# Chunked attention and a gated feed-forward block: eleven small copies behind one sigmoid, and two subtractions in another place of the plan

## The chip, the cores and the metric

The kernel runs on one core of a Trainium2 chip. The metric is the device time of one execution in microseconds (us), the median of several runs. TensorE is written PE (its weight loads PEld), VectorE DVE, ScalarE ACT, GpSimd POOL, and the queue that issues the transfers SP.

## The reference: what is computed

Attention within chunks of 64 tokens (8 batches, 8 heads, 576 tokens, heads of 64), and behind it a gated feed-forward block on 4608 tokens with 512 features and 1536 hidden features, all in 32-bit floats:

```
scores = scale * matmul(q_c, k_c^T);  scores -= max(scores)
attn = exp(scores) / (sum(exp(scores)) + 1e-9);  x = matmul(attn, v_c)
out = (sigmoid(x @ w_gate) * (x @ w_val)) @ w_out
```

The weights arrive as 64-bit floats and are converted on the chip.

## The kernel before, in words

The 4608 tokens are nine blocks of 512. Every matrix product is made of three products of reduced-precision parts: each operand is split into a high part (a rounded copy) and a low part (the difference from it), and high·high, high·low and low·high are added up. Block 0 and the conversion of the weights follow a list written out by hand. Blocks 1 and 2 are worked by `rest` (line 893), one hidden slice of 128 features after the other: `step` calls `hidden` (line 369), and `finish` calls `down` for the slice before. Blocks 3 to 8 are worked two at a time by `pairs` (line 915), where a scheme of seven products takes the place of eight, so that sums and differences of the input tiles are needed (`differ`, line 508, and `operands`, line 515).

In one slice of blocks 1 and 2 PE does twelve matmuls for the gate (bank g0), twelve for the value (bank g1), and twelve of `down` for the slice before. Gate and value have the same name, g, and the same line 356 in the profile. Behind the gate ACT takes the sigmoid into hf (L372); behind the value DVE multiplies (L375), ACT rounds the product into hx (L378), and DVE writes the low part of hx (L380). The gate of the next slice can begin only when the sigmoid has read g0, its value only when the multiplication has read g1.

Beside this runs the attention of later blocks. It is a generator, `flow` (line 757), whose pieces `tick` lets out one by one. A piece is bought with credit, and some wait on a word: "apart" holds the generator while the tick's place is "middle", and where blocks are not yet joined in pairs also until a tick after the one at which the word came up; "piece" holds it for a tick in a like way. A pass of the attention on two heads goes: scores on PE (sc, L196), the maximum and the subtraction on DVE (L782, L783), the exponential on ACT (L787, which changes ACT's table before and after it), sum, reciprocal and product on DVE (L805 to L810), two transposes on DVE (L814). The transposed 32-wide blocks are then put in place by sixteen copies (L825, pr to pt): every third one is POOL's, at once, and the other eleven are ACT's. In blocks 1 and 2 these eleven are not written at once but put on a list, `held`, and `release` writes them out. When all sixteen are there, PE multiplies them with the values (av, L211). `release(5)` writes the first five of the list, `release()` up to sixteen.

Engines run their instructions in the order in which they are written. That order is fixed by hand for all engines in blocks 0 to 2 but for POOL and SP in part, and for PE and POOL in the pairs, where the compiler's scheduler sets the others. During blocks 1 and 2 POOL and DVE also make sums of weight parts (a_val, a_high, L451 to L465), which SP writes to memory for the pairs.

In the pairs a product pair is `first` (products into cx and cy, then s1u = cy + copy of cx on DVE, L568), `last` of the pair before (L622, L625), and `middle` (L601, L607, and the multiplications L578). Product 7 of `middle` adds into the same bank cy that L568 reads. Product 5 of `middle` is written to bank g0 (cz), the bank that L622 of the pair before has to read first.

Of the kernel before, what the change touches and what calls it, by code (L numbers as in the profile page):

```python
# [68 lines left out]
def chunk_attn_moe(ctx: ExitStack, tc: tile.TileContext, q, k, v, w, out, outt):  # L69
# [278 lines left out]
    def up(m, f, which, tok):  # L348
        ps = ps_g.tile([P, TB], F32, tag=f"g{which}", name=f"g{which}", bufs=1)
        n = 0  # L350
        for u in range(2):
            x = xt[m, u]
            for i in range(2):
                c = (2 * u + i) * P
                for wpart, part in ((0, 0), (0, 1), (1, 0)):
                    nc.tensor.matmul(  # L356
                        ps[:, tok], lhsT=wt[f, which][:, wpart, c:c + P], rhs=x[:, part, i, tok],
                        start=n == 0, stop=n == 11)
                    n += 1
        return ps[:, tok]  # L360
# [3 lines left out]
    def release(most=16):  # L364
        for one in held[:most]:
            one()
        del held[:most]

    def hidden(m, f, tok):
        pg = up(m, f, 0, tok)  # L370
        hf = mp.tile([P, TB], F32, name="hf", bufs=1)[:, tok]
        nc.scalar.activation(hf, pg, AF.Sigmoid)  # L372
        release(5)
        pv = up(m, f, 1, tok)
        nc.vector.tensor_tensor(out=hf, in0=pv, in1=hf, op=ALU.mult)  # L375
        both = mp.tile([P, 2, TB], F32R, name="hx")
        hh, hl = both[:, 0], both[:, 1]
        nc.scalar.copy(hh[:, tok], hf)  # L378
        release()
        nc.vector.tensor_tensor(out=hl[:, tok], in0=hf, in1=hh[:, tok].bitcast(F32), op=ALU.subtract)  # L380
        return m, f, tok, hh, hl
# [126 lines left out]
    def differ(n):  # L508

        for (u, b), (u0, b0), (u1, b1) in (((0, 1), (0, 1), (0, 0)), ((1, 1), (1, 1), (0, 1))):  # L510
            yield 1.2
            nc.vector.tensor_tensor(
                out=raw[n, u][:, :, b], in0=raw[n, u0][:, :, b0], in1=raw[n, u1][:, :, b1], op=ALU.subtract)

# [242 lines left out]
    def flow():  # L757
# [3 lines left out]
        for j in range(8, 4 * NB + 2, 2):  # L761
# [34 lines left out]
            if n > 0 and rest == 0:  # L796
                yield from differ(n - 1)
                yield ("early", n - 1)
                yield from operands(n - 1)
                yield ("up", n - 1)  # L800
# [76 lines left out]
    def step(m, f, span):  # L877
        pending.append(hidden(m, f, spans[span]))
# [114 lines left out]
```

## Time and profile before

| | |
|---|---|
| runs | 901.86, 905.09, 906.74 us, median 905.09 |
| the profiled execution | 902.03 us, of which 900.2 us lie between its first and its last instruction |
| PE busy | 98% of the span; DVE 69%, ACT 46%, POOL 30% |
| PE's granted clock | 0.996 of full speed over the span |
| blocks 1 and 2 | from about 150 to 357 us |
| the three pairs | from about 357 us on |

A matmul's duration in the trace overlaps the next one's, so a stretch of PE is read by the distance between starts. "Idle before" in brackets is the time the engine stood still before the row, with the instruction that ended it.

### The profile page before, as it was taken

The numbers are of one execution on the slowest core, as the hardware profiler recorded it, in microseconds if no ns is written. First come the engines' busy times: TensorE is split into PE (matmuls) and PEld (weight loads), VectorE is DVE, ScalarE is ACT, GpSimd is POOL, SyncE is SP. The second block draws the span as 40 slices with busy tenths as digits, with TensorE's granted clock in tenths as the row PEclk, the third lists the DMA queues.
The fourth block names the chain that finished last, engine by engine and source line by source line (L and its number), as shares of the span: only waits on it lengthen the run. The fifth ranks groups of instructions, "written<-read, shape, count | busy, mean of one in ns | idle before, by whom it ended". The sixth has DMA issues, their size and how long they took to land.

```text
span 900.2 us, 15612 instructions
## 1 busy us (share of the span) xinstructions
PE 882.1 (98%) x6054; PEld 720.3 (80%) x6054; DVE 618.8 (69%) x882; ACT 412.0 (46%) x738; POOL 272.4 (30%) x337
## 2 busy tenths in 40 slices
PE   7999999999999999999999999999999999999998
PEld 4887788887877878888888888887788888888886
DVE  6999882586665966666658976666679853435884
ACT  7887672355524463355544524455246221122341
POOL 0000000397846990267750001253500002432000
PEclk9999999999998999999999999999999999999999
DMA  8899962336354475588775567665446685564553
GB/s 312 305 338 297 353 195 71 131 129 190 131 166 148 142 221 177 171 278 284 257 277 187 210 231 283 234 234 190 163 160 224 211 283 197 183 204 150 187 210 117
DMA packets 84506, 189.77 MB, mean 211 GB/s; under 512 B 7248, under 2 KB 45648, under 8 KB 80592
## 3 DMA queue, kind: packets, MB, share of 16 engines
q1 hardware_dynamic: 84432, 188.77, 61.2%
q8 instruction: 48, 0.79, 0.4%
q14 instruction: 26, 0.21, 0.1%
HBM read 146.28 MB, written 42.47 MB: 210 GB/s over the span
## 4 chain that ended last, share of the span: by engine, by line
PE 81%; DVE 7%; ACT 4%; POOL 3%; issue 2%; DMA 2%; SPq 0%; POOLq 0%; DVEq 0%; ACTq 0%
PE d L699 19%; PE g L356 16%; PE cy L550 15%; PE cx L550 11%; PE cz L550 10%; PE acc L391 7%; PE av L211 2%; PE sc L196 2%; DMA w_raw<-w_in 2%; POOL pt L825 1%; ACT early L263 1%; ACT pt L825 1%; POOL a_val L465 1%; DVE xc L540 1%; DVE w_raw L153 1%
## 5 line engine op out<-in xcount | busy, mean ns | idle before, releaser
L356 PE MATMUL g<-xt,w 128*128 128x512 f32 (+1 forms) x960 | 208.1, 372 | 1.0 <-ACT hf L312 0.5
L356 PEld LDWEIGHTS g<-xt,w 128*128 128x128 f32 x960 | 168.5, 190 | 34.1 <-ACT hf L312 1.5
L699 PE MATMUL d<-hd,wd 128*128 128x512 f32 x756 | 172.5, 389 | 0.1
L699 PEld LDWEIGHTS d<-hd,wd 128*128 128x128 f32 x756 | 141.7, 188 | 30.3 <-DVE hd L679 0.9
L550 PE MATMUL cy<-xc,wr 128*128 128x512 f32 x648 | 159.4, 389 | 1.2 <-DVE s1u L568 1.2
L550 PEld LDWEIGHTS cy<-xc,wr 128*128 128x128 f32 x648 | 121.6, 188 | 26.8 <-DVE s1u L568 1.6
L550 PE MATMUL cx<-xc,wr 128*128 128x512 f32 x432 | 111.0, 392 | 0.6 <-issue 0.6
L550 PE MATMUL cz<-xc,wr 128*128 128x512 f32 x432 | 110.0, 390 | 0.2
L391 PE MATMUL acc<-w,hx 128*128 128x512 f32 x432 | 106.7, 394 | 0.1
L550 PEld LDWEIGHTS cz<-xc,wr 128*128 128x128 f32 x432 | 80.9, 188 | 17.8 <-issue 1.0
L550 PEld LDWEIGHTS cx<-xc,wr 128*128 128x128 f32 x432 | 80.5, 188 | 18.0 <-issue 1.0
L391 PEld LDWEIGHTS acc<-w,hx 128*128 128x128 f32 x432 | 79.7, 188 | 17.7 <-DVE hx L322 0.8
L825 POOL COPY pt<-pr 32x256 f32<-32x256 f32 x94 | 39.7, 423 | 163.9 <-DVE pr L814 154.8
L460 POOL TENSOR_TENSOR a_val<-a_val 128x128 f32<-128x128 f32 x36 | 19.0, 527 | 217.9 <-DVE a_val L451 167.5
L678 ACT CAST hd<-hid 128x1024 fp32r<-128x1024 f32 x48 | 49.9, 1052 | 49.2 <-PE d L699 33.2
L566 ACT COPY s1u<-cx 128x512 f32<-128x512 f32 x36 | 21.1, 587 | 106.3 <-PE cx L550 106.3
L679 DVE TENSOR_TENSOR hd<-hid,hd 128x1024 fp32r<-128x1024 f32 x48 | 58.3, 1221 | 12.4 <-ACT hd L678 12.2
L578 POOL TENSOR_TENSOR hid<-u,hid 128x512 f32<-128x512 f32 x15 | 19.3, 1285 | 142.4 <-DVE u L607 141.7
L825 ACT COPY pt<-pr 32x256 f32<-32x256 f32 x130 | 52.4, 403 | 10.5 <-DVE pr L814 8.6
L568 DVE TENSOR_TENSOR s1u<-cy,s1u 128x512 f32<-128x512 f32 x36 | 24.7, 685 | 39.9 <-PE cy L550 35.4
L628 ACT ACTIVATE hid<-hid 128x512 f32<-128x512 f32 x54 | 32.4, 628 | 35.3 <-DVE hid L622 29.3
L578 POOL TENSOR_TENSOR hid<-s1u,hid 128x512 f32<-128x512 f32 x30 | 41.1, 1379 | 20.8 <-DVE s1u L622 20.2
(118 smaller groups left out, 1118.4 us busy)
## 6 DMA issues: line engine op xcount, KB each, us to landing
wr<-sums SPq DMA_DIRECT2D x72, 512.0 KB, 4.8
wd<-stream SPq DMA_DIRECT2D x30, 1024.0 KB, 4.6
w_raw<-w_in SPq DMA_DIRECT2D x36, 512.0 KB, 5.2
wr<-given SPq DMA_DIRECT2D x36, 512.0 KB, 3.8
qt<-q_in SPq DMA_DIRECT2D x18, 512.0 KB, 4.8
kt<-k_in SPq DMA_DIRECT2D x18, 512.0 KB, 5.7
vt<-v_in SPq DMA_DIRECT2D x18, 512.0 KB, 4.7
given<-w SPq DMA_DIRECT2D x36, 256.0 KB, 5.6
```

The costliest lines, as they stand in the source:

```text
L356: nc.tensor.matmul(ps[:, tok], lhsT=wt[f, which][:, wpart, c:c + P], rhs=x[:, part, i, tok], start=n == 0, stop=n == 11)
L391: nc.tensor.matmul(acc[m, t], lhsT=hx[:, ts], rhs=wt[f, 2][:, wpart], start=f == 0 and i == 0, stop=f == NF - 1 and i == 2,)
L460: nc.gpsimd.tensor_tensor(out=val[:, 1], in0=val[:, 1], in1=val[:, 2], op=ALU.add)
L550: nc.tensor.matmul(bank, lhsT=lhs(wpart, c), rhs=x[:, part, c], start=start and k == 0, stop=stop and k == 5, skip_group_check=True)
L566: nc.scalar.copy(s1, x)
L568: nc.vector.tensor_tensor(out=u2, in0=y, in1=s1, op=ALU.add)
L578: eng.tensor_tensor(out=h, in0=value, in1=h, op=ALU.mult)
L628: nc.scalar.activation(h, h, AF.Sigmoid)
L678: nc.scalar.copy(t[:, 0], at)
L679: nc.vector.tensor_tensor(out=t[:, 1], in0=at, in1=t[:, 0].bitcast(F32), op=ALU.subtract)
L699: nc.tensor.matmul(bank, lhsT=w[:, o:o + P], rhs=x[:, part], start=p == 0 and opening and i == 0, stop=p == 5 and i == 2, skip_group_check ...
L825: copy = (lambda eng, dst=pb[dst, :, c, i, :], src=ps[src, h::2, k, :]: eng(dst, src))
```

## The change

Two edits. In `hidden` the call behind the sigmoid releases the whole list instead of five copies; the call behind the rounding of hx stays and finds the list empty. In `differ` each of the two subtractions is held at places named "middle", and where blocks are not joined (the first pair's) also for one tick more.

```diff
@@ hidden(m, f, tok)
         nc.scalar.activation(hf, pg, AF.Sigmoid)
-        release(5)
+        release()
         pv = up(m, f, 1, tok)
         nc.vector.tensor_tensor(out=hf, in0=pv, in1=hf, op=ALU.mult)
...
@@ differ(n)
             yield 1.2
+            yield "apart"
             nc.vector.tensor_tensor(
                 out=raw[n, u][:, :, b], in0=raw[n, u0][:, :, b0], in1=raw[n, u1][:, :, b1], op=ALU.subtract)
```

The added line moves every later line of the file down by one. The order of instructions is the same on PE, POOL and SP. On ACT the copies move in six places, which look alike. One of them, in block 1, before the change; "pt<-pr" are the copies, "hx<-hf" is the rounding, L787 the exponential:

```order
L372 ACTIVATE hf<-g_2341 128x512
L825 COPY pt<-pr 32x8x32 x5
L378 CAST hx<-hf 128x512
L825 COPY pt<-pr 32x8x32 x6
L787 ACT_TABLE_LOAD
L787 ACTIVATE pr<-pr 128x1024
```

and the same place after it:

```order
L372 ACTIVATE hf<-g_2341 128x512
L826 COPY pt<-pr 32x8x32 x11
L378 CAST hx<-hf 128x512
L788 ACT_TABLE_LOAD
L788 ACTIVATE pr<-pr 128x1024
```

Six copies go from behind the rounding of hx to ahead of it.

On DVE the first pair's subtractions (L512) stand at the end of block 2 among the multiplications of its last slices (L375) and the work on the pair's operands (L528, L540). Before the change:

```order
L375 TENSOR_TENSOR hf<-g_3684,hf 128x512
L380 TENSOR_TENSOR hx<-hf,hx 128x512
L512 TENSOR_TENSOR raw<-raw 128x2x512 x2
L540 TENSOR_TENSOR xc<-raw,xc 128x1024 x3
L528 TENSOR_TENSOR raw<-raw 128x2x512
L375 TENSOR_TENSOR hf<-g_3754,hf 128x512
L380 TENSOR_TENSOR hx<-hf,hx 128x512
L540 TENSOR_TENSOR xc<-raw,xc 128x1024 x2
L528 TENSOR_TENSOR raw<-raw 128x2x512 x2
L375 TENSOR_TENSOR hf<-g_3806,hf 128x512
L380 TENSOR_TENSOR hx<-hf,hx 128x512
L540 TENSOR_TENSOR xc<-raw,xc 128x1024 x2
```

and after it:

```order
L375 TENSOR_TENSOR hf<-g_3684,hf 128x512
L380 TENSOR_TENSOR hx<-hf,hx 128x512
L513 TENSOR_TENSOR raw<-raw 128x2x512
L375 TENSOR_TENSOR hf<-g_3741,hf 128x512
L380 TENSOR_TENSOR hx<-hf,hx 128x512
L513 TENSOR_TENSOR raw<-raw 128x2x512
L541 TENSOR_TENSOR xc<-raw,xc 128x1024 x3
L529 TENSOR_TENSOR raw<-raw 128x2x512
L541 TENSOR_TENSOR xc<-raw,xc 128x1024 x2
L529 TENSOR_TENSOR raw<-raw 128x2x512
L375 TENSOR_TENSOR hf<-g_3803,hf 128x512
L380 TENSOR_TENSOR hx<-hf,hx 128x512
```

The second subtraction and what follows it come behind one more multiplication, and eight operations on whole operand tiles now stand between two multiplications, where four and four stood. ACT's roundings of these tiles move with them: five in a row ahead of a sigmoid, where four stood ahead of the sigmoid of one slice before.

The second pair's subtractions keep their place. The third pair's, on DVE in the last products of the second pair, before the change:

```order
L601 TENSOR_TENSOR u_6585<-cy,s1u_6480 128x512
L607 TENSOR_TENSOR hid<-cz,u_6585 128x512
L512 TENSOR_TENSOR raw<-raw 128x2x512 x2
L568 TENSOR_TENSOR s1u_6605<-cy,s1u_6605 128x512
L622 TENSOR_TENSOR hid<-cz,s1u_6480 128x512
```

and after it:

```order
L602 TENSOR_TENSOR u_6585<-cy,s1u_6480 128x512
L608 TENSOR_TENSOR hid<-cz,u_6585 128x512
L569 TENSOR_TENSOR s1u_6603<-cy,s1u_6603 128x512
L513 TENSOR_TENSOR raw<-raw 128x2x512 x2
L623 TENSOR_TENSOR hid<-cz,s1u_6480 128x512
```

Both subtractions go from ahead of the addition of `first` to behind it.

## Rows read from the trace of the kernel before

**Rows 1.** Page, busy us (share of the span) and instructions.
```profile
PE 882.1 (98%) x6054; PEld 720.3 (80%) x6054; DVE 618.8 (69%) x882; ACT 412.0 (46%) x738; POOL 272.4 (30%) x337
```
**Rows 2.** PE's waits: who for, us in total, times, longest us.
```profile
PE av L211 <- ACT pt L825: 5.6, 6, 3.8
...
PE cy L550 <- DVE s1u L568: 1.2, 1, 1.2
```
**Rows 3.** Windows: length, busy us of PE, PEld, DVE, ACT, POOL, clock, DMA share, GB/s.
```profile
268.00:270.00 2.00, 0.00 (x1) 0.00 (x0) 1.38 (x2) 0.58 (x1) 1.48 (x4) 1.00 0.53 179
...
274.00:276.00 2.00, 2.00 (x18) 1.59 (x11) 0.28 (x1) 1.99 (x5) 1.84 (x4) 0.50 0.42 139
```
**Rows 4.** Timeline, 263 to 282 us: start, us, engine, instruction, idle before.
```profile
263.90 2.07 ACT L825 COPY pt<-pr 32x256 f32<-32x256 f32 x5
...
267.66 0.34 PE L211 MATMUL av<-pt,vt 64*64 64x64 f32 x8
...
268.70 0.68 DVE L375 TENSOR_TENSOR hf<-g,hf 128x512 f32<-128x512 f32 x1
...
274.29 7.59 PE L356 MATMUL g<-xt,w 128*128 128x512 f32 x24
...
281.71 2.88 PE L391 MATMUL acc<-w,hx 128*128 128x512 f32 x12
```
**Rows 5.** Timeline, 316 to 332 us, ACT and PE.
```profile
316.29 2.07 ACT L825 COPY pt<-pr 32x256 f32<-32x256 f32 x5
...
321.12 0.34 PE L211 MATMUL av<-pt,vt 64*64 64x64 f32 x8
...
322.49 1.04 PE L211 MATMUL av<-pt,vt 64*64 64x64 f32 x54 [0.45 <-ACT pt L825]
...
329.03 2.88 PE L391 MATMUL acc<-w,hx 128*128 128x512 f32 x12
```
**Rows 6.** Timeline, PE where nothing waits, 294 to 300 us.
```profile
293.91 5.60 PE L356 MATMUL g<-xt,w 128*128 128x512 f32 x24
...
299.44 1.16 PE L211 MATMUL av<-pt,vt 64*64 64x64 f32 x64
```
**Rows 7.** Timeline, 227 to 241 us, ACT and PE.
```profile
227.35 2.07 ACT L825 COPY pt<-pr 32x256 f32<-32x256 f32 x5
...
230.21 0.62 ACT L378 CAST hx<-hf 128x512 fp32r<-128x512 f32 x1 [0.79 <-DVE hf L375]
...
237.01 0.60 ACT L372 ACTIVATE hf<-g 128x512 f32<-128x512 f32 x1
...
240.09 5.60 PE L356 MATMUL g<-xt,w 128*128 128x512 f32 x24
```
**Rows 8.** Timeline, 635 to 645 us, DVE, POOL and PE.
```profile
635.07 5.35 DVE L512 TENSOR_TENSOR raw<-raw 128x1024 f32<-128x1024 f32 x2
...
635.62 1.52 PE L550 MATMUL cy<-xc,wr 128*128 128x512 f32 x6
...
636.08 3.26 POOL L643 TENSOR_TENSOR hid<-hid 128x1024 f32<-128x1024 f32 x1
...
640.34 0.68 DVE L568 TENSOR_TENSOR s1u<-cy,s1u 128x512 f32<-128x512 f32 x1
...
643.95 1.52 PE L550 MATMUL cz<-xc,wr 128*128 128x512 f32 x6
```
**Rows 9.** All subtractions of line 512: ns min/median/max, first and last start.
```profile
L512 DVE TENSOR_TENSOR raw<-raw x6: 1216/1824/3248, 331.3 to 637.2; 128x1024 f32<-128x1024 f32 x6
```
**Rows 10.** Timeline, 335 to 349 us, DVE, PE and ACT.
```profile
335.20 5.00 DVE L540 TENSOR_TENSOR xc<-raw,xc 128x1024 fp32r<-128x1024 f32 x3
...
337.19 2.88 PE L391 MATMUL acc<-w,hx 128*128 128x512 f32 x12
...
347.72 0.58 ACT L372 ACTIVATE hf<-g 128x512 f32<-128x512 f32 x1
...
348.36 5.78 PE L356 MATMUL g<-xt,w 128*128 128x512 f32 x24
```

## The prediction, made before the run

> **What bounds the kernel now.** First the page's line of busy times: PE is busy 98% of the span [rows 1]. So the kernel is PE's work plus the few places where PE stands still, and an edit on ACT or DVE is worth only the PE time it frees or costs. Next I read PE's waits. The largest is av on the copies pt that ACT writes, 5.6 us in six pieces, one of 3.8; near it is cy on the addition s1u, 1.2 us [rows 2]. These are the two things the edits touch. Then the clock by windows. At 268 us PE still has its upper level (1.00, 2.4 GHz) but does nothing for 2 us; at 274 us, after the long wait, it works at 0.50, that is 1.2 GHz [rows 3]. So the 3.8 us wait has a second price. Last come the timelines of the places where the order changes.
>
> **The six places of copies.** A copy on ACT takes 2.07 / 5 = 0.414 us [rows 4]; eleven in one go take 4.55.
>
> Long stall. The first five start at 263.90. The other six stand behind the rounding of hx, which needs DVE's multiplication at 268.70, and so start after 270. PE has begun av at 267.66, does the part for which copies are there, and stops [rows 4]. From the start of av to the next `down` at 281.71 are 14.05 us. With nothing in the way this stretch is gate and value, 299.44 - 293.91 = 5.53 us [rows 6], and av, 1.16 us: 6.7 us. The stall with its slow tail costs 7.4 us. After the change the copies end at 263.90 + 4.55 = 268.45, so av still waits a little: its last part of 54 matmuls starts at about 268.5, takes 1.0 (322.49 row, at full clock) [rows 5], the gate starts near 269.5, `down` near 275.0. Gain 281.71 - 275.0 = **6.7 us**. About 2 of them come from the clock (24 matmuls in 7.59 instead of 5.60 us) and a little more from av at half speed. The wait left for av is about 0.4 us in one piece; the waits of 0.45 us in rows 5 are followed by av and gate at full speed, so I take the clock to stay up. If it fell all the same, the gain would be 4.5.
>
> Two short stalls of one form. At 321.12 PE starts av, and `down` follows at 329.03: 7.91 us for the stretch that takes 6.7 undisturbed, so 1.2 us lost [rows 5]. The copies began at 316.29, so eleven end at 320.84, ahead of av. The other, near 212 in block 1, has the same form and the same 7.91 us, and its copies too would end just ahead of av. Gain 2 × 1.2 = **2.4 us**.
>
> The other three places have no stall to lose. What the edit adds there is a later hx. At the tightest, eleven copies end at 227.35 + 4.55 = 231.9, and hx starts there instead of 230.21: 1.7 us late [rows 7]. Queued behind it are, on ACT, the exponential with its two table loads and then the next sigmoid; on DVE, the low part of hx, maxima and subtractions, whose result the exponential needs. So the sigmoid at 237.01 ends up to 1.7 us late, at 239.3. Who waits for it is the gate that starts at 240.09: it is still covered by 0.8 us [rows 7]. The two others have the same form and a longer cover. `down` reads hx a whole gate and value later. Cost 0; if a shift came out at 3 us, it would cost under 1 us a place.
>
> **The third pair's subtractions.** Both stand before L568 and take 5.35 us beside POOL's work on hid (L643, 3.26 us) [rows 8]; so L568 comes at 640.34, and PE's cy has waited 1.2 us for it [rows 2]. After the change L568 follows cy's first product (635.62 + 1.52), ends near 637.9, and that wait is gone. What is late next is L622, now behind the subtractions; cz, which started at 643.95 [rows 8], would come 1.2 us earlier, at 642.7, and needs L622's bank. Two subtractions take 2.4 us at their shortest (1216 ns) [rows 9], then L622 ends at 637.9 + 2.4 + 0.7 = 641.0 and nothing waits; at 5.35 us it ends at 643.9, and PE waits at cz what it saved at cy. I take **1.2 us**, since POOL's L643 began at 636.08 and would run without DVE's subtractions beside it until 637.9, so most of it is over by then; the range is 0 to 1.2.
>
> Here a rule bears on the choice. The two subtractions took 5.35 us, the longer of them 3.25, where the shortest of all takes 1.2, and they ended 1.1 us after POOL's L643, about the length of a short one [rows 8, 9]. The Trainium skill ("SBUF — State Buffer", section "Who interferes with whom") says that a DVE instruction with two inputs in SBUF blocks against a GpSimd instruction that reads SBUF: whichever comes second waits for the whole of the other. By that rule the moved subtractions wait for the end of L643, at 639.3 at the latest, and end by 641.8; L622 ends at 642.5, in time for cz, and the term stays 1.2. By a reading in which both just run slower side by side, they could take the 5.35 us again, and the term is 0. The rows before fit the rule.
>
> **The first pair's subtractions.** The second one and what follows move behind one more multiplication. Eight whole-tile operations now lie between two multiplications. The `down` at 337.19 marks the end of a value; the multiplication, rounding and low part take 2.1 us, so the eight start at 339.3. At the shortest length, 1.22 us each [rows 9], they end at 349.1 and the next multiplication at 349.8. The value matmuls that need its bank start 2.7 us behind the gate of 348.36, at 351 [rows 10]. Cover 1.2 us. If the L540 stay as slow as before (5.00 us for three, 1.3 more than at the shortest) the cover is gone, and a second such lengthening costs 1 to 2 us. On the other side the gate at 348.36 has waited some 0.3 us for the sigmoid at 347.72 behind a rounding [rows 10]; that wait can go. I take **0**, between -2 and +0.3.
>
> **Sum.** 6.7 + 2.4 + 1.2 + 0 = 10.3 us. The profiled execution took 902.03 us, so the same execution would take 891.7. The median of the runs is 905.09, 3 us above the profiled one; from there it is 894.8. I predict the middle, **893 us**.
>
> **Rivals.** (1) The stalls shorten, but the clock still falls at 268, or cz waits for L622, or both: the gain is 10.3 - 2.2 - 1.2 = 7 us, 896 to 898. For it: a wait of 0.4 us is left there, beside small av matmuls. Against: the same form at 321 keeps its speed [rows 5].
> (2) The squeeze at the end of block 2 decides: the multiplications of the last three slices come late one after another, PE waits about 2 us for g1 twice, the third pair's term is lost too: gain 5, 898 to 900. For it: DVE's three L540 took 5.00 us [rows 10]; against: POOL's sums, which lengthen them, are over by then.
> (3) Slower: hx behind eleven copies delays the next sigmoid at all six places by more than the row's cover. The cover is 240.09 - 237.61 = 2.5 us [rows 7]; from a shift of 2.5 us on PE waits for g0. To be slower the six waits must exceed 10.3 us, so 1.8 each and a shift of 4.3; at 5 us each it is 15 - 10 = 5 us slower, about 909. Against: the copies move hx by 1.7, and then nothing is added on ACT, since six copies fewer follow it.
> (4) The change does nothing measurable: PE comes out ahead but DVE and POOL, with their sums of weights, set the pace of block 2 and hand the time back, 901 to 905. Against: over the span PE is busy 98%, DVE 69% and POOL 30% [rows 1].
>
> **How the numbers follow.** Forecast 0.72, rival 1 0.12, rival 2 0.08, rival 3 0.04, rival 4 0.04. The likeliest case alone spans 889 to 896.5, by its terms' bounds and the 3 us between the execution and the median. The range, 887 to 900.5, adds rivals 1 and 2. A difference under 0.5% (4.5 us, so above 900.6) can't be told from no change; faster has 0.89 (the forecast, rival 1 and most of rival 2), the same 0.07, slower 0.04.
>
> **What would show it.** In PE's waits, av on pt falls from 5.6 us to under 1, and cy on s1u is gone. The clock stays at 1.00 from 268 to 280 us. The stretch from av to `down` is near 7.3 us at the long stall and 6.7 at the two others. The rounding of hx starts about 1.7 us later behind eleven copies, and no gate gains a wait on the sigmoid. At the end of block 2 no value waits on L375, and cz doesn't wait for L622. The prediction is wrong if PE's freed time shows up as waits of gate or value on ACT or DVE in block 2, or if the clock falls somewhere else.

## The result, and the profile after

The changed kernel takes 894.34 us (median of 4 runs, 893.44 to 897.39) beside 905.48 us for the kernel before (4 runs, 901.86 to 906.74): a ratio of 0.9894 on record, with a 95% interval of 0.9860 to 0.9928 (the two medians alone divide to 0.9877, inside it). It is faster, by 1.1%. The profiled execution of it took 893.44 us, with 891.7 us between first and last instruction.

Page of the changed kernel: busy us, share and instructions of each engine, and the clock granted to PE in 40 slices.

```profile
PE 878.5 (99%) x6054; PEld 718.0 (81%) x6054; DVE 616.3 (69%) x882; ACT 412.2 (46%) x738; POOL 268.4 (30%) x337
...
PEclk9999999999999999999999999999999999999999
```

The instructions are the same in number as in [rows 1]; PE is busy 3.6 us less (a matmul at half clock counts as busy) and the span is 8.5 us shorter.

PE's waits in the changed kernel: who for, us in total, times, longest us.

```profile
PE cx L551 <- issue: 1.4, 1, 1.4
...
PE av L211 <- ACT pt L826: 0.4, 1, 0.4
PE cz L551 <- DVE u L608: 0.3, 2, 0.2
```

Of the 5.6 us for ACT's copies 0.4 are left, and cy no longer waits for s1u [rows 2]. Two small ones are new: cz for u, 0.3 us in two pieces, neither of them in the third pair, and not there in the kernel's two repeats; and g for L375 (the multiplication), 0.2 us at 260.80 us in block 2, 0.3 in the first repeat and not listed in the second. The largest of this list, cx for "issue", has no releaser in the profile; it is taken up at the end.

The long place, the changed kernel's timeline (start, us, engine, instruction, idle before), to be laid beside [rows 4]:

```profile
262.73 4.57 ACT L826 COPY pt<-pr 32x256 f32<-32x256 f32 x11
...
266.46 0.44 PE L211 MATMUL av<-pt,vt 64*64 64x64 f32 x10
...
267.35 1.04 PE L211 MATMUL av<-pt,vt 64*64 64x64 f32 x54 [0.44 <-ACT pt L826]
267.52 0.68 DVE L375 TENSOR_TENSOR hf<-g,hf 128x512 f32<-128x512 f32 x1
...
268.31 5.73 PE L356 MATMUL g<-xt,w 128*128 128x512 f32 x24
...
273.88 2.88 PE L391 MATMUL acc<-w,hx 128*128 128x512 f32 x12
```

The eleventh copy ends at 267.30, before DVE's multiplication has even begun, and av goes on at 267.35. From av to `down` it is 273.88 - 266.46 = 7.42 us, where it was 14.05. Gate and value, 24 matmuls, take 5.73 us instead of 7.59. The windows of this place (columns as in [rows 3]) show why:

```profile
268.00:270.00 2.00, 2.00 (x33) 1.67 (x25) 1.31 (x3) 1.75 (x2) 1.78 (x4) 1.00 0.42 139
...
274.00:276.00 2.00, 2.00 (x11) 1.65 (x10) 1.06 (x2) 0.84 (x2) 2.00 (x5) 1.00 0.00 0
```

PE is busy all through, and the granted clock stays at 1.00, the level of 2.4 GHz.

The third pair, timeline of the changed kernel, to be laid beside [rows 8]:

```profile
628.57 1.52 PE L551 MATMUL cy<-xc,wr 128*128 128x512 f32 x6
...
629.02 2.40 POOL L644 TENSOR_TENSOR hid<-hid 128x1024 f32<-128x1024 f32 x1
...
630.20 0.69 DVE L569 TENSOR_TENSOR s1u<-cy,s1u 128x512 f32<-128x512 f32 x1 [2.10 <-PE cy L551]
630.81 2.96 DVE L513 TENSOR_TENSOR raw<-raw 128x1024 f32<-128x1024 f32 x2
...
633.69 0.68 DVE L623 TENSOR_TENSOR hid<-cz,s1u 128x512 f32<-128x512 f32 x1
...
635.37 1.52 PE L551 MATMUL cz<-xc,wr 128*128 128x512 f32 x6
```

The addition (L569) now comes right behind cy's product, the subtractions take 2.96 us in place of 5.35, L623 ends at 634.37, and cz starts at 635.37 without a wait.

To see what each edit does, the distance between the same two PE instructions is read in each trace. The starts that name a stretch are those of the kernel before; "block 2's end" runs from the `down` at 329.03 to the one at 356.69, the third pair from cy at 635.62 to cx at 642.57. "Copies only" and "subtractions only" are two of the experiments below, "repeat" is the changed kernel profiled once more.

| us | before | changed | repeat | copies only | subtractions only | predicted change |
|---|---|---|---|---|---|---|
| short place at 212, av to `down` | 7.91 | 6.67 | 6.67 | 6.67 | 7.91 | -1.2 |
| long place, av to `down` | 14.06 | 7.42 | 7.45 | 7.44 | 13.04 | -6.7 |
| short place at 321, av to `down` | 7.91 | 7.10 | 7.09 | 6.67 | 7.92 | -1.2 |
| block 2's end | 27.66 | 27.20 | 27.20 | 28.03 | 27.20 | 0 |
| third pair, cy to cx | 6.95 | 5.44 | 5.44 | 6.95 | 5.44 | -1.2 |
| sum of the five | 64.49 | 53.83 | 53.85 | 54.76 | 61.51 | -10.3 |

The five stretches gain 10.66 us in the changed kernel and 10.64 in its repeat. The span shortened by 8.5: in that one execution some 2 us came back elsewhere, the most of it between 357 and 610 us (1.21) and at the wait for "issue" (0.80). In the repeat the stretch between 357 and 610 is 253.40 us, as before (253.48), so the 1.21 belong to one execution and not to the kernel.

One entry of the table needs a word. Subtractions only leaves the copies split, and its long place waits as long as before (3.85 us), yet it takes 13.04 us and not 14.06: gate and value took 6.92 us there, not 7.59, and the window from 276 to 278 us has a clock of 0.71, where the kernel before shows 0.50. So the same wait cost 1.0 us more in one execution than in the other, by the clock alone. The 6.6 us gained against the profile of before would be 5.6 against this one.

### The profile page after: what moved, and what is told of

The parts are those of the page before. It is cut to its first block, busy times and chain, and to the rows that moved or that the text cites. A ratio compares the mean times of both kernels' runs of the same rounds, so it can differ in the third digit from the quotient of the medians.

```text
span 891.7 us, 15611 instructions
## 1 busy us (share of the span) xinstructions
PE 878.5 (99%) x6054; PEld 718.0 (81%) x6054; DVE 616.3 (69%) x882; ACT 412.2 (46%) x738; POOL 268.4 (30%) x337
## 4 chain that ended last, share of the span: by engine, by line
PE 76%; DVE 10%; ACT 5%; DMA 3%; POOL 3%; issue 3%; SPq 1%; POOLq 0%; DVEq 0%; ACTq 0%
PE d L700 19%; PE cy L551 14%; PE g L356 13%; PE cx L551 10%; PE cz L551 10%; PE acc L391 7%; DMA w_raw<-w_in 2%; PE av L211 2%; POOL pt L826 1%; ACT pt L826 1%; PE sc L196 1%; DVE pr L811 1%; DVE sums L806 1%; ACT early L263 1%; DVE w_raw L153 1%
## 5 line engine op out<-in xcount | busy, mean ns | idle before, releaser
L569 DVE TENSOR_TENSOR s1u<-cy,s1u 128x512 f32<-128x512 f32 x36 | 24.7, 685 | 42.0 <-PE cy L551 37.5
```

What stands on the lines that cost most here:

```text
L569: nc.vector.tensor_tensor(out=u2, in0=y, in1=s1, op=ALU.add)
```

## The experiments

**The changed kernel again.**

> The changed kernel once more, as the mark for the three others on the same chip. Theory: 0.990 of the kernel before; a second profile shows the same stretches of PE at the long place and at the two short ones within 0.3 us, and where the two executions of this kernel differ: at 21 to 27 us (the clock) and around 605 us (a wait of PE without a releaser), by up to 2 us together. Rival (the runs differ by transfers all over the span): the differences are spread over many places, none above 0.5 us.

Measured: 893.32 us (6 runs), ratio 0.9902 [0.9883, 0.9922]. All five stretches are within 0.03 us of the first profile (table). The clock was at its upper level at 21 to 27 us in both profiles; the wait without a releaser was 0.2 us instead of 1.4.

**Copies only.**

```diff
-        release(5)
+        release()
```

> The whole list of copies is released behind the sigmoid; the subtractions stay where they were before. Theory (PE is the bound, each stall is worth its own length): the long stall gives 6.5 us (2.2 of them the clock), the two short ones 2 us together, so 8.5 us or 0.9905 of the kernel before; PE's wait of cy for s1u stays at 1.2 us, the clock stays at full speed from 268 to 280 us. Rival (the freed time is handed back by DVE and POOL in the later blocks, and only the two edits together show): under 5 us, above 0.9945.

Measured: 896.30 us (5 runs) beside 903.65 for the kernel before (23 runs), ratio 0.9922 [0.9907, 0.9937], so 7.0 us and not 8.5. Its waits of PE:

```profile
PE cy L550 <- DVE s1u L568: 1.2, 1, 1.2
...
PE g L356 <- ACT hf L372: 0.5, 1, 0.5
PE av L211 <- ACT pt L825: 0.4, 1, 0.4
```

The waits for copies go with this edit alone, the wait of cy stays, and a gate's wait of 0.5 us for a sigmoid at the end of block 2 shows up.

**Subtractions only.**

```diff
             yield 1.2
+            yield "apart"
```

> Only the subtractions move; the copies stay split five and six. Theory: 1.4 us at the third pair (cy no longer waits 1.2 us for s1u, cz waits for nothing) and 0.3 us at the end of block 2, so about 1.7 us, 0.998. Rival (the wait moves from cy to cz, and eight tile operations between two multiplications cost PE time): 0 to 2 us slower, 1.000 to 1.002, with cz or the value matmuls waiting.

Measured: 901.72 us (12 runs), ratio 0.9977 [0.9965, 0.9990]. The copies' wait is all there:

```profile
PE av L211 <- ACT pt L826: 5.8, 6, 3.9
```

No wait of cy or cz is left in the third pair. By the ratios this edit is worth 0.23% and the copies 0.78%; together 1.01%, where the three measurements of both gave 1.06, 0.98 and 0.89%. Within the noise the two edits add up. In its profile the five stretches gain 2.98 us, of which 1.0 is the clock at the long place, with which the edit has nothing to do.

**All eleven copies at the long place only.**

```diff
-        release(5)
+        release(16 if (m, f) == (2, 2) else 5)
```

> The whole list is released behind the sigmoid only at the one place with the long stall; the five other places and the subtractions are as before. Theory: 6.5 us (wait 4.3, clock 2.2), 0.993; the two short stalls of 1.2 us are still there. Rival (each of the six places gives about the same, since what counts is that six copies fewer stand between the rounding and the exponential): 1.5 us, 0.998.

Measured: 898.55 us (6 runs), ratio 0.9951 [0.9934, 0.9968], so 4.4 us and not 6.5. The long place itself gained all that was expected (7.44 us for the stretch, 6.62 less). But the next place, which keeps the split, got worse: 9.05 us instead of 7.91, and the end of block 2 took 0.41 more; so 5.1 are left by these stretches. The timeline of that next place in this run:

```profile
313.59 0.90 DVE L458 TENSOR_TENSOR a_val<-w 128x128 f32<-128x128 f32 x2
...
314.41 0.68 DVE L375 TENSOR_TENSOR hf<-g,hf 128x512 f32<-128x512 f32 x1
...
315.82 0.34 PE L211 MATMUL av<-pt,vt 64*64 64x64 f32 x8
...
317.56 0.29 PE L211 MATMUL av<-pt,vt 64*64 64x64 f32 x2 [1.40 <-ACT pt L825]
```

PE arrives earlier, DVE's sums of weights (L458) don't, and the multiplication queues behind them; with it come the rounding, the last six copies, and av. A part of freed PE time is spent waiting for an engine that was not freed. By the ratio neither the 6.5 us nor the rival's 1.5 came.

**PE kept busy while it waits.** The kernel before, with 22 matmuls more of 128x512 into g0 ahead of the av of the long place. Their result is read by nothing.

```diff
+        if j == 14:
+            idle = ps_g.tile([P, TB], F32, tag="g0", name="idle", bufs=1)
+            for _ in range(22):
+                nc.tensor.matmul(
+                    idle, lhsT=blank[:, :P], rhs=blank[:, P:].unsqueeze(1).broadcast_to([P, 4, P]), start=True, stop=True)
```

> The kernel before, with 22 matmuls of 128x512 in bf16 that nothing reads (0.216 us each, 4.75 us in all) written into the free bank g0 ahead of av at the long stall: PE still loses the time that it waited for the copies, but is busy meanwhile. Theory (part of the price is the clock): the clock stays at 1.00 from 268 to 280 us, and from the start of what was av (267.66) to the next down 4.75 + 6.69 = 11.4 us pass where 14.05 did: 2.6 us faster, 0.997. Rival (the wait alone is the price, or the clock falls whatever PE does there): the same time or up to 1 us slower, 1.000 to 1.001.

Measured: 903.94 us (12 runs), ratio 1.0007 [0.9995, 1.0020]. PE's timeline at the place:

```profile
269.72 4.92 PE L206 MATMUL idle<-ident 128*128 128x512 bf16 x22
...
274.57 1.22 PE L216 MATMUL av<-pt,vt 64*64 64x64 f32 x64
...
281.31 2.88 PE L396 MATMUL acc<-w,hx 128*128 128x512 f32 x12
```

The copies come as late as before, but av takes 1.22 us and the gate 5.74 us at full clock. Between the `down` before and the one behind, it is 281.31 - 267.00 = 14.31 us, where the kernel before needs 16.86: the half clock cost 2.55 us there. Against the subtractions-only profile, whose clock came back sooner, it is 15.85 - 14.31 = 1.54 us. The whole time, however, did not fall. The short place after it lost 0.7 us to a longer wait for copies, as in the run before, and the wait for "issue", 0.6 us at 612 us in the kernel before, was now 2.3 us and at 432 us, and the stretch from 19 to 96 us, with the clock at half speed at 22 us, took 78.7 us in place of 76.8. So the price of the clock is shown where it arises, and not as a gain in the total.

**Ten copies behind the sigmoid, one behind the rounding.**

```diff
-        release()
+        release(10)
```

> The changed kernel, but ten copies are released behind the sigmoid and one behind the rounding of hx. Theory (av waits for the last copy, and that copy stands behind the late multiplication, however few stand there): the last copy at the long place ends about 1.9 us later than in the changed kernel, so PE waits some 2.4 us there in place of 0.4, and the kernel is 2 us slower than the changed one, 4 if the clock falls too: 0.992 to 0.994 of the kernel before. Rival (each copy behind the rounding costs a sixth of the gain): 1.4 us slower than the changed kernel, spread over three places, with at most 1.1 at the long one.

Measured: 896.51 us (6 runs), ratio 0.9934 [0.9912, 0.9955]. Timeline of the long place:

```profile
265.69 4.16 ACT L826 COPY pt<-pr 32x256 f32<-32x256 f32 x10
...
271.85 0.40 ACT L826 COPY pt<-pr 32x256 f32<-32x256 f32 x1
...
272.30 1.04 PE L211 MATMUL av<-pt,vt 64*64 64x64 f32 x54 [2.40 <-ACT pt L826]
```

One copy of 0.40 us behind the rounding holds 54 matmuls for 2.40 us. So most of the stall is set by where the last copy stands; the five more that came late in the kernel before add their own time (the waits there are 3.84 and 0.30 us). The stretch took 9.39 us, 2.0 more than with none late, where the rival had at most 1.1; the two short places lost 0.33 and 0.35 us besides. And behind an idle time of 2.40 us the granted clock is 1.00 (windows, columns as in [rows 3]),

```profile
274.00:276.00 2.00, 2.00 (x10) 1.62 (x10) 2.00 (x3) 1.98 (x6) 1.56 (x3) 1.00 0.38 131
```

where behind 3.8 us it was 0.50 [rows 2, 3]. That is no border between the two: the next run has a stop of 2.34 us with 0.50 behind it (last section).

**Half of the copies on POOL**, to take away the last 0.4 us of wait.

```diff
-                if n % (2 if now["joined"] else 3) == 1:
+                if n % 2 == 1:
```

> The changed kernel, with every second of the sixteen copies on POOL also in blocks 1 and 2: eight and eight in place of eleven and five. Theory (ACT's last copy is what av still waits for): ACT's copies take 3.3 in place of 4.55 us, the last 0.4 us of waiting at the long place go, 0.4 to 0.8 us faster than the changed kernel, which is hard to tell from none. Rival (POOL's copies stand in line with its sums of weights and come last): av waits for POOL, 1 to 3 us slower than the changed kernel.

Measured: 896.73 us (12 runs), ratio 0.9941 [0.9923, 0.9958]: 3.4 us slower than the changed kernel beside it (893.32 us), in the direction of the rival; its profile has a wait for "issue" of 2.3 us besides. The long place falls to 6.67 us, its undisturbed length, but POOL is now late elsewhere (av waits 1.0 us for it at the short place at 321, which takes 7.99), and a `down` waits:

```profile
PE acc L391 <- DVE ob L409: 1.5, 1, 1.5
```

**More filling matmuls in the opening.** In several profiles above the clock fell at 22 us; this run adds matmuls there that are read by nothing. (The lines are of the list written out by hand for block 0.)

```diff
-... w.1.2 t.1.0 fill.17 turn.0.1
+... w.1.2 t.1.0 fill.24 turn.0.1
-... exp.1.1 av.0 d.1.0 ...
+... exp.1.1 fill.5 av.0 d.1.0 ...
```

> The changed kernel, with 12 more matmuls that nothing reads in the opening, where PE waits for the transposes (1.5 us) and for av (1.25 us) at 17.5 to 21.3 us: 7 more ahead of the first transposes, 5 ahead of the first av. In four of six profiled executions the clock was at half speed from about 21 to 27 us, which cost 1.3 to 2.2 us there; in the other two it stayed up. Theory (PE's idle time just before decides, and the executions differ in whether the clock falls): the clock stays at 1.00 from 18 to 30 us, the median is 1 to 2 us under the changed kernel's and the runs spread less. Rival (these matmuls only fill time that other work sets, and the spread comes from the transfers): the same median within 0.5 us; since 24 more instructions move the points at which PE's program is fetched, a wait without a releaser may move and cost up to 2 us.

Measured: 892.20 us (5 runs, 891.46 to 897.68), ratio 0.9888 [0.9866, 0.9911]. It is 1.1 us under the changed kernel beside it, with intervals that overlap, so the gain is not shown; the runs spread by 6.2 us, not less than that kernel's 3.5. The opening keeps 1.00, but the profiled execution, at 897.68 the longest of the five, lost the time at 606 us, where PE stood 2.8 us without a releaser:

```profile
606.35 0.34 PE L196 MATMUL sc<-kt,qt 64*64 64x64 f32 x7 [2.81 <-issue]
```

**The same, with the rest of PE's program shifted.** 37 small matmuls (128x128, `pad`) and 2 fills in place of the 12 added fills; with their weight loads these are 78 PE instructions more than in the changed kernel (the lines that define `pad` are left out here).

```diff
-... t.1.0 fill.17 turn.0.1
+... t.1.0 fill.17 pad.25 turn.0.1
-... exp.1.1 av.0 d.1.0 ...
+... exp.1.1 fill.2 pad.12 av.0 d.1.0 ...
```

> The changed kernel, with 39 matmuls that nothing reads in PE's two idle stretches of the opening (25 small ones ahead of the first transposes, 2 large and 12 small ones ahead of the first av): PE is busy there, and all its later instructions stand 78 places further on in its program. In the profiles so far PE's wait without a releaser came after those bursts of av and scores that begin 182, 185 or 206 places behind a multiple of 256, and not, or not over 0.6 us, after those at 3, 40, 64, 81, 141, 218 and 226; 78 places on, the seven double bursts of the pairs begin at 4, 40, 81, 118, 142, 159 and 219. Theory (PE waits there for its own program, which comes in pieces of 16 KB, and for the clock in the opening): no wait without a releaser above 0.6 us, the clock at 1.00 over the whole span, 1 to 2.5 us faster than the changed kernel on the same chip, and no run over 895. Rival (the wait belongs to the place at 605 us, to its transfers, and the clock of the opening is chance): the wait stays there, between 0.2 and 2.3 us, and the median is within 0.7 us of the changed kernel's.

Measured: 893.34 us (4 runs), ratio 0.9903 [0.9887, 0.9920]. The wait for "issue" is gone in its profile, the clock is 1.00 over the span, and no run is over 895. As two kernels without the shift have no such wait either (last section), this does not show what the shift does.

**The changed kernel a third time**, beside the run above.

> The changed kernel, as the mark for the other on the same chip: 0.990 of the kernel before.

Measured: 894.59 us (4 runs), ratio 0.9911 [0.9896, 0.9926]. The intervals overlap, so the 1.25 us between these two don't show that the shifted program is faster. No version measurably beat the changed kernel.

## Why the prediction was right

The forecast was the case that came: 893.0 us against 894.34, and 893.3 and 894.6 in the two repeats.

**The bound.** PE bound the kernel, and the gain is PE's waits and PE's clock. Copies only, with ACT's order changed and nothing else, gave three quarters of it by the ratios, and 9.7 of 10.7 us by the stretches.

**The long place.** 6.7 us were forecast, 6.64 measured. The steps came one by one: eleven copies in 4.57 us, 0.44 us of wait left, then 54 matmuls in 1.04, the gate at full clock. Two experiments split the sum. With PE busy during the wait the place gave back 2.55 us, the share of the clock in the profile of before (the forecast said about 2, and a little more for av); in the subtractions-only profile that share is 1.5. The forecast worked from one execution and was measured against the same one: that the sizes meet within 0.1 us is in part luck, for against the other profile the place gained 5.6. With one copy left behind the rounding the place took 9.39 us, 2.0 more than with none. Rival 1 is out: the clock is 1.00 in every window from 266 to 280 us, and cz does not wait for L622's bank.

**The short places.** The one at 212 gave 1.24 us as forecast. The one at 321 gave 0.81. This is the term that was too large. The prediction took the copies to begin as long before av as they did (321.12 - 316.29 = 4.8 us); they begin 4.1 us before it. Timeline of the changed kernel:

```profile
304.98 1.57 DVE L458 TENSOR_TENSOR a_val<-w 128x128 f32<-128x128 f32 x2
...
306.47 0.68 DVE L375 TENSOR_TENSOR hf<-g,hf 128x512 f32<-128x512 f32 x1
...
308.78 0.60 ACT L372 ACTIVATE hf<-g 128x512 f32<-128x512 f32 x1 [0.98 <-DVE hx L380]
...
309.28 4.57 ACT L826 COPY pt<-pr 32x256 f32<-32x256 f32 x11
...
313.36 1.57 PE L211 MATMUL av<-pt,vt 64*64 64x64 f32 x64
```

The multiplication stands behind the sums of weights. The next sigmoid writes hf, which the low part of hx (L380, the releaser in its row) has to read first, so sigmoid and copies are late, and the copies end at 313.85, inside av. In the copies-only run av waited for nothing here (6.67), although the order on DVE and POOL is the same up to this place. Counted from av, DVE's rows of the two runs lie within 0.1 us until they part at one pair of instructions that start within 0.02 us of each other, first the changed kernel, then copies only:

```profile
275.63 1.85 DVE L380 TENSOR_TENSOR hx<-hf,hx 128x512 fp32r<-128x512 f32 x1 [0.69 <-ACT hx L378]
275.64 1.29 POOL L465 TENSOR_TENSOR a_val<-a_val,a_high 128x512 f32<-128x512 f32 x1
```

```profile
276.80 0.69 DVE L380 TENSOR_TENSOR hx<-hf,hx 128x512 fp32r<-128x512 f32 x1 [0.69 <-ACT hx L378]
276.82 1.81 POOL L465 TENSOR_TENSOR a_val<-a_val,a_high 128x512 f32<-128x512 f32 x1
```

One of the two takes its own 0.69 or 1.29 us, the other that much and most of the first one's besides. In the changed kernel it is DVE that comes second, and it stays 1.2 us behind up to the multiplication (L375): this starts 6.89 us ahead of av, 8.09 in copies only, 10.47 before. DVE came second in all five profiles with this order on ACT and DVE (the changed kernel's three and the two with matmuls added in the opening; 1.85 to 1.87 us), and there the stretch took 7.09 to 7.12. So DVE is late here by two amounts: 2.4 us that came with PE's freed time, and alone cost nothing in copies only, and 1.2 from POOL. In the run with the long place only DVE came second too (1.86 us); with PE kept busy while it waited DVE did not, and 0.7 us were lost all the same. Rival 4 (DVE and POOL hand the time back) was right in kind, and 0.4 us in size.

**The places that had no stall.** Three of the six places had none to lose, and lost next to none. At the tightest, timeline of the changed kernel beside [rows 7]:

```profile
225.84 4.56 ACT L826 COPY pt<-pr 32x256 f32<-32x256 f32 x11
...
230.43 0.63 ACT L378 CAST hx<-hf 128x512 fp32r<-128x512 f32 x1
...
237.15 0.60 ACT L372 ACTIVATE hf<-g 128x512 f32<-128x512 f32 x1
...
238.75 3.56 PE L356 MATMUL g<-xt,w 128*128 128x512 f32 x15
```

hx starts 4.59 us behind the first copy where it was 2.86: 1.7 us later, as forecast. The sigmoid ends at 237.75 and the gate starts at 238.75: a cover of 1.0 us is left, forecast 0.8. Rival 3 is out by that 1.0 us. The prediction called itself wrong if PE's freed time showed up as waits of gate or value in block 2. One such wait came, the 0.2 us for L375 at 260.80 us (0.3 in the first repeat): right in kind as a warning, and too small to change the sum.

**The third pair.** 1.51 us gained against 1.2 forecast. The row of the wait shows 1.2, the distance between starts fell by 1.5. A row's idle time counts from the drawn end of the matmul before, and a group of six is drawn 1.52 us long where the next starts after 1.36: 0.16 of the 0.3 are that, so a wait costs a little more than its row shows. The choice between the ends of this term was for the higher one, from L643's early start, and in keeping with the rule of the Trainium skill ("SBUF — State Buffer", section "Who interferes with whom") that one of a DVE instruction with two SBUF inputs and a GpSimd instruction that reads SBUF waits out the other. The trace agrees: L644, now first, takes 2.40 us (3.26 before, when a subtraction was ahead of it); it ends at 631.42, and the first subtraction, begun at 630.81, ends at 632.5, 1.1 us behind it, near the length of a short subtraction (1.2 us).

```profile
L513 DVE TENSOR_TENSOR raw<-raw x6: 1215/1227/1699, 322.8 to 632.5; 128x1024 f32<-128x1024 f32 x6
```

The longest of the six is now 1.70 us (3.25 before [rows 9]).

**The first pair.** 0 was forecast, between -2 and +0.3; the end of block 2 gained 0.46, so rival 2 (a squeeze there) is out. Timeline of the changed kernel:

```profile
332.01 3.56 DVE L541 TENSOR_TENSOR xc<-raw,xc 128x1024 fp32r<-128x1024 f32 x3
...
338.97 1.22 DVE L529 TENSOR_TENSOR raw<-raw 128x1024 f32<-128x1024 f32 x1
...
339.50 5.60 PE L356 MATMUL g<-xt,w 128*128 128x512 f32 x24
340.10 0.68 DVE L375 TENSOR_TENSOR hf<-g,hf 128x512 f32<-128x512 f32 x1
```

The eight whole-tile operations ran at their shortest (3.56 us for three, 5.00 before [rows 10]). The multiplication ends at 340.8, and the value matmuls begin half way through the 5.60 us of gate and value, near 342.2. The cover is 1.4 us, forecast 1.2. What was gained is the gate's wait for the sigmoid, which the prediction named as the better end: with copies only it is there (0.5 us, 28.03), with the subtractions only it is gone (27.20).

**From the terms to the time.** The five terms sum to 10.66 us measured, 10.3 forecast. The runs say somewhat less: ratios of 0.9894, 0.9902 and 0.9911 are 9.6, 8.9 and 8.0 us of 903.65, the median of 23 runs of the kernel before. What lies between is not in the terms, or is the clock at the long place, 1.0 us apart in the two profiles that have that wait: the wait for "issue" was 1.4 and 1.6 us in two profiles of the changed kernel and 0.2 in the other, 0.6 in the one of before, and the stretch from 19 to 96 us took 77.1, 77.7 and 79.4 us in its three profiles (76.8 before). The base was mis-sized too: the prediction took the profiled execution of before to lie 3 us under the median, and against the medians beside the experiments it is 1.6 (23 runs), 0.1 (17) and 0.6 (7). So a part of the agreement within 1.3 us is chance; the terms are what was shown.

## What to carry to other kernels

A queue that is emptied in two parts around an instruction that waits for another engine delivers its last piece at that engine's time: one copy of 0.4 us on the wrong side cost 2.4 us. A wait on PE may be followed by matmuls at half clock, so read the windows behind a wait as well as the wait. When PE is made faster, list what then comes before it on the engines that were not: the freed time goes first to those, here 0.4 us of it, and 1.1 us where only one of the places was mended. And where two engines hold each other up, which of them starts first, here by 0.02 us, can decide whether a cover of a microsecond is there or not.

## What the runs showed of the hardware

**A wait without a releaser, at one place of the program.** In nine of the twelve profiles PE stops once or twice in or behind a dense run of 64x64 matmuls (av and sc) with nothing in the rows that it waits for. Changed kernel:

```profile
601.30 1.11 PE L196 MATMUL sc<-kt,qt 64*64 64x64 f32 x64
...
605.13 0.50 PE L551 MATMUL cx<-xc,wr 128*128 128x512 f32 x1 [1.35 <-issue]
```

It is 0.6 us in the kernel before, 1.4, 0.2 and 1.6 in three profiles of the changed one, and up to 2.8 in the others. Three have none over 0.15 us: the kernel with 78 PE instructions more, and also subtractions only and the long place only, whose PE program is that of before. So its absence need not be the work of the shift. Where it comes is counted in instructions: in six profiles 4753 matmuls stand ahead of it, and 4753 again with 12 matmuls added in the opening, which is 12 matmuls earlier in the work (4750 with half of the copies on POOL); with 22 added in block 2 it came at 432 us behind 3505, and the run with 12 added has a second, of 0.4 us, behind 3504.

The page of the changed kernel (queue: packets, MB, share of 16 engines) has

```profile
q8 instruction: 48, 0.79, 0.3%
```

and the traces hold these packets one by one, 16 KB each. At all ten stops that are over 0.15 us PE goes on 1.2 to 1.5 us after one of these packets has landed: at 605.13 in the changed kernel, with the packet landed at 603.77; at 612.17 in the kernel before, at 610.67. In the two profiles of the same program without a stop the packet had landed earlier, 2.1 and 2.3 us before the same matmul. That is what would be seen if PE waits for the next piece of its own program where instructions are brief. It is shown by these times alone: no run brought the program in another way.

**The clock in the opening.** Two executions of the changed kernel, the windows at 22 us, first the third profile and then the second:

```profile
22.00:24.00 2.00, 2.00 (x49) 1.33 (x44) 1.53 (x3) 1.53 (x4) 0.00 (x0) 0.50 1.01 408
```

```profile
22.00:24.00 2.00, 2.00 (x19) 0.88 (x10) 1.55 (x5) 1.78 (x6) 0.00 (x0) 1.00 1.02 414
```

PE has stood 1.5 and 1.2 us shortly before, in both. The clock is 0.50 there in 6 of the 12 profiles, and from 19 to 96 us these take 77.7 to 79.7 us, the four others without added matmuls 76.8 to 77.7; in both kernels with more matmuls in the opening it was 1.00. Behind single stops it was 0.50 after 3.84 us (before), after 2.81 (more fills, at 606 us) and after 2.34 (half of the copies on POOL, at 607 us), and 1.00 after 2.40 us (ten copies) and after 2.35 (PE kept busy, at 432 us). The opening's shorter stops too went with either, so the length of one stop does not tell.
